# A fused attention, gated convolution and spatial-gating kernel: two token tiles of batch 1 are loaded in long rows and transposed by TensorE, the rest in 32 small loads, under a new order

## The chip, the cores and the metric

One core of a Trainium2 chip. The metric is the device time of one execution in microseconds (us); for the kernel before it is given as the median of three runs. One more execution of it was profiled, and every duration below is from that one.

## The reference

q, k and v are (4, 8, 576, 64) in batch, head, token and head dimension. Three layers follow one another, all in fp32:

```python
scores = scale * np.matmul(q, k.transpose(0, 1, 3, 2))
mask = (rel >= 0) & (rel < 64)          # rel = query position - key position
attn = softmax(np.where(mask, scores, -1000000000.0))
x = np.matmul(attn, v)                  # heads joined: (4, 576, 512)

h = np.maximum(x @ w_in, 0.0)           # 512 -> 1024
conv_out = 3-tap convolution of h along the tokens
x = (h * sigmoid(conv_out)) @ w_out     # 1024 -> 512

h = np.maximum(x @ w2_in, 0.0)          # 512 -> 1024, split into u and v
v_s = np.einsum('ts,bsd->btd', w_spatial, layernorm(v)) + b_spatial[None, :, None]
out = (u * v_s) @ w2_out                # 512 -> 512
```

## The kernel before

Products are done in three matmuls each, of high and low parts of the two factors. The work comes in this order of stages, which overlap:

- Attention runs in 18 rounds (`rec_round`), each of two blocks of 64 queries; batch 0 has blocks 0 to 8, so round 4 holds the last block of batch 0 and the first of batch 1. A round is: scores `s` (L625; in the first six rounds the mask is added by two matmuls of L620), row maxima on DVE, exponentials on ACT (L654), normalisation, transposes `pt` (L684) and their copies `pts`, and `pv` (L717), whose result is split into the high and low parts `xc`.
- The 2304 tokens of x form six chunks of 384. Chunk c needs rounds up to 3c + 2. For each there are eight groups `h` (L810 to L812, 12 matmuls of 386 or 388 columns each) and eight groups `y` (L882 to L884). w_in and w_out come in blocks through two `raw` buffers and are converted on DVE and ACT.
- The second layer follows in the last part, batch by batch; there `gr` is multiplied (L1186 on DVE, L1189 on POOL).

q and k must lie with the head dimension on partitions. Batch 0 gets there by `rec_load_first` and `rec_qk_first`: a tile of 128 tokens is loaded in rows of 256 B into a stage buffer `qk` (five of them; four issues of 128 KB for q and k), and TensorE transposes it (four matmuls `tr` of L556 for q and four for k), with a copy out of PSUM for each. Batches 1 to 3 use `rec_load_qk` (L533): eight loads of 288 KB, in pieces of 128 B, followed by 32x32 transposes on DVE (`rec_qk`, L570), two for each pair of blocks. v comes in windows of 128 tokens (`rec_load_v`, L544), into three buffers `vw`.

Nothing is written in program order. Each `op` has a rank, a cost for each engine that may do it, and at times an earliest time `at`; the class `Plan` runs a list schedule over these numbers and emits the instructions in the order that comes out, which is then fixed for each engine's queue. DMAs are all issued by SP, in that order too, and an issue whose buffer is not free holds up those behind it. The ranks come from the table `PLAN`. The earliest time is the last argument here:

```python
op(rank + 0.1 * g, {"D": 2.5}, ld, w=[(nm, b, "ld", g)], b=[dst[b]], at=rank)
```

`bias(k, t)` weighs the engines against each other by two times, TE1 and TE2, of the schedule.

Of the kernel before, what the change touches and what calls it, by code (L numbers as in the profile page):

```python
# [20 lines left out]
PLAN = {  # L21
    "BP": 0.532,
    "BP1": 0.052,
    "BP2": 2.886,
    "BV": 1.453,
    "BV1": 2.001,
    "BV2": 2.211,
    "CS": 1.104,
    "CW": -3.463,
    "CWL": 0.128,  # L30
    "DC": 1.72,
    "G2S": -0.157,
    "G2": 5.836,
    "LAT": 0.209,
    "LD0": 3.993,
    "LD": 1.243,
    "LEAD": 1.994,
    "PORT": 0.05,
    "QK": -1.46,
    "QL": 0.083,  # L40
    "QL1": -7.091,
    "QV": 1.784,
# [22 lines left out]
    "wo0": 7.827,
    "wo1": -9.101,
    "wo2": -13.346,
    "wo3": 15.676,
    "wo4": -39.117,
    "wo5": -20.38,  # L70
    "wo6": 10.642,
    "wo7": 8.186,
    "r0": -5.237,
    "r1": 29.482,
    "r2": -6.678,
    "r3": -1.91,
    "r4": -2.742,
    "r5": -40.242,
    "r6": 7.708,
    "r7": 7.596,  # L80
    "r8": -0.104,
    "r9": -4.244,
    "r10": -0.595,
    "r11": -29.119,
    "r12": -9.391,
    "r13": -0.755,
    "r14": -10.067,
    "r15": -19.207,
    "r16": -13.345,
    "r17": -2.471,  # L90
# [161 lines left out]
def tile_attention_convglu_spatial(  # L252
# [261 lines left out]
    def rec_load_first(t, rank):  # L514
# [33 lines left out]
    def rec_qk_first(t, rank):  # L548
        n = min(P, S - t * P)
        for j, (nm, dst) in enumerate((("q", qT[0]), ("k", kT[0]))):  # L550
            a = stage[t]
# [5 lines left out]
            key = (nm, "tr", t)  # L557
            op(rank, {"T": 0.46}, tr, r=[("qk0", t, j), "ident"], w=[key], b=[a, pt_])
# [3 lines left out]
                r=[key], w=[(nm, 0, 2 * t + i) for i in range(n // W)], b=[pt_, dst],  # L562
            )

    def rec_qk(b, i, n, rank):

        for nm, dst in (("q", qT[b]), ("k", kT[b])):
            def tr(e, dst=dst):
                d = dst()[:, :, i * W:(i + n) * W]
                nc.vector.transpose(out=d, in_=d.rearrange("p h (u c) -> p h u c", c=32))  # L570
            op(
                rank, {"V": c_tt(n * W * HP)}, tr,
                r=[(nm, b, "ld", g) for g in range(4)], w=[(nm, b, i + j) for j in range(n)], b=[dst],
            )
# [29 lines left out]
    def rec_round(p, rank):  # L604
# [134 lines left out]
    def rec_conv(rank, load, n, issues=1, lead=PLAN["LD"], ring=None):  # L739

        raw = ring or mk(p2, [P, n, 2], I, "raw", "raw", 2)
# [5 lines left out]
        op(rank - lead, {"D": PLAN["DC"]}, lambda e: load(raw()), w=[(key, "raw")], b=[raw], issues=issues)  # L747
# [24 lines left out]
    def rec_w_in(f, rank):  # L772
# [6 lines left out]
        get, own, key, _ = rec_conv(rank, ld, KD * P, issues=2, lead=PLAN["LD0"] if f < 2 else PLAN["LD"])  # L779
# [150 lines left out]
    for t in range(NT):  # L930
        rec_load_first(t, t_block(0, 2 * t) - (PLAN["QL1"] if t else 12.0))
# [6 lines left out]
    for t in range(NT):  # L938
        rec_qk_first(t, t_block(0, 2 * t) - PLAN["QK"])
# [378 lines left out]
```

## Time and profile before

| | |
|---|---|
| median of 3 runs | 532.07 us (531.66 to 533.03) |
| profiled execution | 535.2 us, of which 533.4 us are the span of its instructions |
| mean granted clock of TensorE | 0.955 |
| busy: PE, DVE, ACT, POOL | 507.0, 348.4, 292.8, 36.6 us (95%, 65%, 55%, 7%) |
| moved by DMA | 67.99 MB, 127 GB/s on average |

PE is TensorE's matmuls, DVE is VectorE, ACT is ScalarE, POOL is GpSimd, and SP is the engine that issues the DMAs; "SPq" in a row is an issue. A busy share is an average over the span. L12 is line 12 of the kernel. The granted clock is a share of TensorE's full 2.4 GHz, so 0.50 is its lower level.

### The profile page before, as it was taken

Reading aid. Unit: us, or ns where it says so; the run is one execution under the profiler, and the core shown is the slowest. Engines: PE = TensorE matmul, PEld = TensorE weight load, DVE = VectorE, ACT = ScalarE, POOL = GpSimd, SP = SyncE. Lnnn points to the kernel's source line nnn. Section 1 sums busy time; section 2 is a strip of 40 time slices with the busy share of each in tenths; the row PEclk is TensorE's granted clock in tenths of the full one; section 3 lists DMA queues with packets and bytes.
Section 4 is the critical chain, followed back from the end, with each engine's and each line's share of the span. In section 5 each row is a group of like instructions: output and inputs, shape, how many; then the busy total and the mean of one; then the engine's idle time right before and its main releaser. Section 6 shows DMA issues by size and latency. Waiting matters only on the chain.

```text
span 533.4 us, 10143 instructions
## 1 busy us (share of the span) xinstructions
PE 507.0 (95%) x3826; PEld 466.5 (87%) x3826; DVE 348.4 (65%) x925; ACT 292.8 (55%) x783; POOL 36.6 (7%) x74
## 2 busy tenths in 40 slices
PE   5774799999999999999999999999999999999997
PEld 4543699999999999999999998998899889988996
DVE  3477899999889888975765428987207820771170
ACT  4576799899878977885544225724220432042111
POOL 3000000000000000000000000051004000400130
PEclk9565699999999999999999999999999999999999
DMA  9999859944997856232346752550222021402003
GB/s 184 168 162 196 202 167 144 205 120 126 156 210 201 247 172 194 60 96 80 80 139 209 254 189 64 178 179 2 79 73 107 0 80 35 163 2 79 1 1 98
DMA packets 133077, 67.99 MB, mean 127 GB/s; under 512 B 106828, under 2 KB 119396, under 8 KB 133028
## 3 DMA queue, kind: packets, MB, share of 16 engines
q1 hardware_dynamic: 133028, 67.35, 52.5%
q8 instruction: 30, 0.49, 0.4%
q14 instruction: 19, 0.16, 0.1%
HBM read 48.98 MB, written 18.35 MB: 126 GB/s over the span
## 4 chain that ended last, share of the span: by engine, by line
PE 89%; SPq 3%; DMA 3%; ACT 3%; DVE 2%; issue 1%; ACTq 0%
PE y L882 7%; PE h L810 7%; PE h L811 6%; PE y L883 6%; PE h L812 6%; PE y L884 6%; PE s L625 4%; PE pv L717 3%; PE sps L1173 3%; PE sps L1172 3%; PE sps L1174 3%; PE ops L1227 3%; PE ops L1225 3%; PE ops L1226 3%; PE vps L1049 3%; PE vps L1051 3%
## 5 line engine op out<-in xcount | busy, mean ns | idle before, releaser
L810 PE MATMUL h<-xc,wi 128*128 128x388 f32 (+1 forms) x192 | 67.5, 351 | 0.0
L882 PE MATMUL y<-g,wo 128*128 128x386 f32 (+1 forms) x192 | 67.3, 350 | 0.0
L842 DVE SCALAR_TENSOR_TENSOR cv<-hs,cw,cv 128x386 f32<-128x386 f32 (+1 forms) x96 | 57.7, 612 | 14.1 <-ACT cv L837 13.7
L811 PE MATMUL h<-xc,wi 128*128 128x388 f32 (+1 forms) x192 | 65.3, 340 | 0.0
L883 PE MATMUL y<-g,wo 128*128 128x386 f32 (+1 forms) x192 | 65.2, 340 | 0.0
L812 PE MATMUL h<-xc,wi 128*128 128x388 f32 (+1 forms) x192 | 65.0, 339 | 0.0
L884 PE MATMUL y<-g,wo 128*128 128x386 f32 (+1 forms) x192 | 64.9, 338 | 0.0
L1186 DVE TENSOR_TENSOR gr<-sps,bb 128x288 f32<-128x288 f32 x32 | 14.6, 457 | 68.7 <-PE sps L1178 67.3
L1110 PE MATMUL ups<-yt,w2i 128*128 128x288 f32 x128 | 38.0, 297 | 0.2 <-DVE ut L358 0.2
L1111 PE MATMUL ups<-yt,w2i 128*128 128x288 f32 x128 | 37.8, 295 | 0.0
L654 ACT ACTIVATE sm<-sm,st 128x128 f32<-128x128 f32 x96 | 37.1, 392 | 1.1 <-DVE st L644 1.1
L882 PEld LDWEIGHTS y<-g,wo 128*128 128x128 f32 x192 | 36.1, 188 | 1.8 <-issue 1.2
L1112 PE MATMUL ups<-yt,w2i 128*128 128x288 f32 x128 | 37.7, 294 | 0.0
L810 PEld LDWEIGHTS h<-xc,wi 128*128 128x128 f32 x192 | 36.2, 188 | 1.0 <-issue 0.5
L884 PEld LDWEIGHTS y<-g,wo 128*128 128x128 f32 x192 | 36.4, 190 | 0.0
L1189 POOL TENSOR_TENSOR gr<-gr,ut 128x288 f32<-128x288 f32 x31 | 26.6, 858 | 141.0 <-DVE gr L1186 140.4
L883 PEld LDWEIGHTS y<-g,wo 128*128 128x128 f32 x192 | 36.2, 189 | 0.0
L811 PEld LDWEIGHTS h<-xc,wi 128*128 128x128 f32 x192 | 36.2, 189 | 0.0
L812 PEld LDWEIGHTS h<-xc,wi 128*128 128x128 f32 x192 | 36.2, 188 | 0.0
L356 ACT ACTIVATE hs<-h 128x388 f32<-128x388 f32 (+1 forms) x45 | 21.7, 490 | 25.7 <-PE h L812 24.9
L684 PE MATMUL pt<-ident,sm 128*128 128x128 f32 x144 | 24.9, 300 | 9.6 <-DVE sm L674 5.0
L684 PEld LDWEIGHTS pt<-ident,sm 128*128 128x128 f32 x144 | 18.9, 153 | 13.0 <-ACT sm L654 5.1
(164 smaller groups left out, 1285.4 us busy)
## 6 DMA issues: line engine op xcount, KB each, us to landing
yt<-yd SPq DMA_DIRECT2D x32, 288.0 KB, 5.2
vw<-in_v_dram SPq DMA_DIRECT2D x32, 256.0 KB, 4.0
raw<-in_moe_w_out_dram SPq DMA_DIRECT2D x12, 512.0 KB, 4.5
raw<-in_moe_w_in_dram SPq DMA_DIRECT2D x16, 256.0 KB, 4.9
raw<-in_moe_w_in_dram SPq DMA_DIRECT2D x8, 512.0 KB, 4.9
w2i<-w2d SPq DMA_DIRECT2D x8, 512.0 KB, 7.1
out_dram<-osb SPq DMA_DIRECT2D x15, 256.0 KB, 2.0
qT<-in_q_dram SPq DMA_DIRECT2D x12, 288.0 KB, 7.0
```

The source lines that it names most:

```text
L654: nc.scalar.activation(out=sm[h]()[:, hp, :], in_=src()[:, hp, :], func=ACTF.Exp, scale=scale if early else -1.0, bias=st()[:, 0, h, hp:hp ...
L684: nc.tensor.transpose(psp[h]()[:, hp, :], sm[h]()[:, hp, :], ident)
L810: mm(hps(), wh, xh, start=(kk == 0), stop=False)
L811: mm(hps(), wh, xl, start=False, stop=False)
L812: mm(hps(), wl, xh, start=False, stop=(kk == KD - 1))
L842: return lambda e: nc.vector.scalar_tensor_tensor(out=cv(), in0=h()[:, j:j + n], scalar=cw[:, j, f:f + 1], in1=cv(), op0=ALU.mult, op1=ALU.add
L882: mm(yps(), wt[:, 0], gt[:, 0, :], start=(kk == 0), stop=False)
L883: mm(yps(), wt[:, 0], gt[:, 1, :], start=False, stop=False)
L884: mm(yps(), wt[:, 1], gt[:, 0, :], start=False, stop=(kk == KF - 1))
L1110: mm(ups(), wt[:, 0], yt[b][0]()[:, kk, o], start=(kk == 0), stop=False)
L1111: mm(ups(), wt[:, 0], yt[b][1]()[:, kk, o], start=False, stop=False)
L1112: mm(ups(), wt[:, 1], yt[b][0]()[:, kk, o], start=False, stop=(kk == KD - 1))
```

## The change

The first two tiles of 128 tokens of batch 1 go the way of batch 0 (`FIRST1 = 2`). The other 320 tokens of batch 1 are loaded head by head, in 32 loads of 40 KB, at the earliest at the rank plus `Q1`; two of the five pairs of DVE transposes of batch 1 fall away. Costs that the schedule counts with are changed (a load of a q and k tile or a v window 1.2 to 1.35, of a batch 2.5 to 2.8, of a w_in block 1.72 to 2.1, the maxima of a late round 1.46 to 0.85). All other numbers of `PLAN` are replaced as well, so that the order changes everywhere; with TE2 at 2057 the bias `BIAS2` holds in the whole schedule, and 31 multiplications of `gr` and three subtractions of w2_out leave POOL. W2 at 181.8 puts the conversions of w2_in at a late rank. The lines of before are found 3 to 17 further down in the code after (L533 as L543 and L548, L556 as L573, L570 as L587, L625 as L642, L684 as L701, L717 as L734, L810 as L827).

```diff
     "DC": 1.72,
...
-    "LD": 1.243,
-    "QK": -1.46,
-    "TE2": 333.331,
-    "W2": 5.115,
...
+    "LD": 7.632,
+    "QK": -0.385,
+    "QL2": 3.737,
+    "QK2": 1.454,
+    "Q1": -0.389,
+    "TE2": 2057.37,
+    "W2": 181.82,
...
+    FIRST1 = 2
+
+    def rec_load_first(b, t, rank):
...
-                        out=a()[:n, j, :, h], in_=src[0, h * HP:(h + 1) * HP, t * P:t * P + n, :].rearrange("h p d -> p h d")
+                        out=a()[:n, j, :, h], in_=src[b, h * HP:(h + 1) * HP, t * P:t * P + n, :].rearrange("h p d -> p h d")
...
-            op(rank + 0.01 * j, {"D": 1.2 * n / P}, ld, w=[("qk0", t, j)], b=[a], issues=2)
+            op(rank + 0.01 * j, {"D": 1.35 * n / P}, ld, w=[("qk0", b, t, j)], b=[a], issues=2)
...
+        t0 = FIRST1 * P if b == 1 else 0
         for nm, src, dst in (("q", q, qT), ("k", k, kT)):
             for g in range(4):
...
+                for hp in range(HP if t0 else 1):
+                    def ld(e, src=src, dst=dst, g=g, hp=hp):
+                        part = src[b, 4 * (g // 2):4 * (g // 2) + 4, :, 32 * (g % 2):32 * (g % 2) + 32]
+                        d = dst[b]()[32 * g:32 * g + 32]
+                        if t0:
+                            nc.sync.dma_start(
+                                out=d[:, hp, t0:].rearrange("p (u c) -> p u c", c=32),
+                                in_=part[hp, t0:].rearrange("(u t) c -> t u c", t=32),
+                            )
+                        else:
+                            nc.sync.dma_start(
+                                out=d.rearrange("p h (u c) -> p (h u) c", c=32), in_=part.rearrange("h (u t) c -> t (h u) c", t=32)
+                            )
+                    op(
+                        rank + 0.1 * g, {"D": 0.45 if t0 else 2.8}, ld, w=[(nm, b, "ld", g, hp)], b=[dst[b]],
+                        at=rank + (PLAN["Q1"] if t0 else 0.0),
                     )
-                op(rank + 0.1 * g, {"D": 2.5}, ld, w=[(nm, b, "ld", g)], b=[dst[b]], at=rank)
...
-            rank, {"D": 1.2},
+            rank, {"D": 1.35},
...
-                rank + 1 * rs + 0.1 * h, {"V": 0.85 if early else 1.46}, mx(h),
+                rank + 1 * rs + 0.1 * h, {"V": 0.85}, mx(h),
...
-        get, own, key, _ = rec_conv(rank, ld, KD * P, issues=2, lead=PLAN["LD0"] if f < 2 else PLAN["LD"])
+        get, own, key, _ = rec_conv(rank, ld, KD * P, issues=2, lead=PLAN["LD0"] if f < 2 else PLAN["LD"], dc=2.1)
...
+    for t in range(FIRST1):
+        rec_load_first(1, t, t_block(1, 2 * t) - PLAN["QL2"])
...
+    for t in range(FIRST1):
+        rec_qk_first(1, t, t_block(1, 2 * t) - PLAN["QK2"])
...
-            if b and i % 2 == 0:
+            if b and i % 2 == 0 and (b > 1 or i >= 2 * FIRST1):
                 rec_qk(b, i, min(2, NB - i), t_round[p] - PLAN["QV"] + 0.1 * i)
```

How the rows of the engines stand now: first PE around rounds 4 and 5, up to the first h of chunk 0. `s` with a mask are scores, `qk_266` and `qk_438` are the two stage buffers of batch 1, and `qk_387` is batch 0's last tile. Before, the rows there are these:

```order
L684 MATMUL pt<-ident,sm 128x128 x4
L620 MATMUL s<-mask_84,ident_r 128x512 x2
L625 MATMUL s<-kT,qT 64x128 x16
L717 MATMUL pv<-pts,vw 64x64 x16
L684 MATMUL pt<-ident,sm 128x128 x8
L717 MATMUL pv<-pts,vw 64x64 x16
L620 MATMUL s<-mask_82,ident_r 128x512 x2
L625 MATMUL s<-kT,qT 64x128 x16
L684 MATMUL pt<-ident,sm 128x128 x4
L810 MATMUL h<-xc,wi_313 128x386
```

and of the change:

```order
L701 MATMUL pt<-ident,sm 128x128 x4
L573 MATMUL tr<-ident,qk_266 128x128 x4
L573 MATMUL tr<-ident,qk_387 128x64 x4
L573 MATMUL tr<-ident,qk_438 128x128 x4
L573 MATMUL tr<-ident,qk_266 128x128 x4
L573 MATMUL tr<-ident,qk_438 128x128 x4
L637 MATMUL s<-mask_84,ident_r 128x512 x2
L642 MATMUL s<-kT,qT 64x128 x16
L734 MATMUL pv<-pts,vw 64x64 x16
L701 MATMUL pt<-ident,sm 128x128 x8
L637 MATMUL s<-mask_82,ident_r 128x512 x2
L642 MATMUL s<-kT,qT 64x128 x16
```

Four groups of batch 1's transposes have come in ahead of round 4's scores. Between the scores of rounds 4 and 5 there stood two pv, of rounds 1 and 2; now there is one, of round 2, since that of round 1 has moved further ahead. The row behind those of the change is the first `h`; the pt that stood ahead of it now stands among chunk 0's h.

Second, PE where chunk 0's h end and chunk 1's begin (386 columns are chunk 0's, 388 chunk 1's). Before:

```order
L810 MATMUL h<-xc,wi_595 128x386
L811 MATMUL h<-xc,wi_595 128x386
L812 MATMUL h<-xc,wi_595 128x386
L810 MATMUL h<-xc,wi_313 128x388
L811 MATMUL h<-xc,wi_313 128x388
L812 MATMUL h<-xc,wi_313 128x388
```

and of the change:

```order
L829 MATMUL h<-xc,wi_746 128x386
L701 MATMUL pt<-ident,sm 128x128 x4
L642 MATMUL s<-kT,qT 64x128 x16
L734 MATMUL pv<-pts,vw 64x64 x16
L701 MATMUL pt<-ident,sm 128x128 x4
L734 MATMUL pv<-pts,vw 64x64 x16
L701 MATMUL pt<-ident,sm 128x128 x4
L642 MATMUL s<-kT,qT 64x128 x16
L701 MATMUL pt<-ident,sm 128x128 x4
L827 MATMUL h<-xc,wi_341 128x388
```

The scores of rounds 6 and 7 (without a mask matmul) and pv of rounds 4 and 5 have moved between the two chunks; before, pv of rounds 4 and 5 stood among chunk 0's h, and the scores of round 6 behind two groups of chunk 1.

Third, SP, the queue of DMA issues, around the last of batch 1's loads. Before:

```order
L533 DMA kT<-in_k_dram 32x72x32
L533 DMA qT<-in_q_dram 32x72x32
L775 DMA raw<-in_moe_w_in_dram 64x4x256 x2
L533 DMA kT<-in_k_dram 32x72x32
L775 DMA raw<-in_moe_w_in_dram 64x4x256 x2
L544 DMA vw<-in_v_dram 128x8x64 x3
L775 DMA raw<-in_moe_w_in_dram 64x4x256 x4
L544 DMA vw<-in_v_dram 128x8x64 x2
L737 DMA raw<-in_moe_w_out_dram 128x1024 x2
```

and of the change, from the v windows that follow pv of round 2 on:

```order
L561 DMA vw<-in_v_dram 128x8x64 x2
L792 DMA raw<-in_moe_w_in_dram 64x4x256 x4
L543 DMA qT<-in_q_dram 32x10x32 x4
L543 DMA kT<-in_k_dram 32x10x32 x4
...
L754 DMA raw<-in_moe_w_out_dram 128x1024 x2
L561 DMA vw<-in_v_dram 128x8x64 x3
```

The eight large loads of batch 1, which began ahead of most of w_in, have become 32 small ones (four times the pair of rows shown) behind all of w_in and behind the v windows that wait for pv of round 2; the window that pv of round 4 reads is the first of the last row.

## Rows read from the trace of the kernel before

**Rows 1.** Busy tenths, clock and DMA in 40 slices of 13.3 us
```profile
PE   5774799999999999999999999999999999999997
...
PEclk9565699999999999999999999999999999999999
...
DMA  9999859944997856232346752550222021402003
```

**Rows 2.** Windows; PEclk is the granted clock, then DMA share and GB/s
```profile
8.00:16.00 8.00, 1.81 (x25) 1.09 (x17) 4.92 (x17) 5.68 (x23) 0.00 (x0) 0.72 1.31 212
...
33.45:40.68 7.23, 5.66 (x44) 3.60 (x43) 5.53 (x16) 5.70 (x27) 0.00 (x0) 0.50 1.41 146
...
60.00:66.00 6.00, 5.91 (x70) 4.59 (x70) 4.83 (x13) 5.78 (x18) 0.00 (x0) 0.50 0.83 242
...
66.00:120.00 54.00, 54.00 (x488) 51.40 (x488) 51.28 (x124) 50.16 (x130) 0.32 (x2) 1.00 0.87 159
...
490.00:533.40 43.40, 40.31 (x271) 37.95 (x269) 11.02 (x28) 7.48 (x18) 6.76 (x8) 1.00 0.11 37
```

**Rows 3.** PE's timeline: start and length in us, line, count, wait before
```profile
14.20 1.09 PE L684 MATMUL pt<-ident,sm 128*128 128x128 f32 x4 [5.01 <-DVE sm L674]
...
19.83 1.11 PE L556 MATMUL tr<-ident,qk 128*128 128x128 f32 x4
...
25.41 1.99 PE L625 MATMUL s<-kT,qT 64*64 64x128 f32 x32
...
33.45 1.99 PE L625 MATMUL s<-kT,qT 64*64 64x128 f32 x32
...
40.68 1.99 PE L625 MATMUL s<-kT,qT 64*64 64x128 f32 x32
...
52.66 2.15 PE L625 MATMUL s<-kT,qT 64*64 64x128 f32 x30 [4.61 <-DVE kT L570]
...
66.52 0.42 PE L810 MATMUL h<-xc,wi 128*128 128x386 f32 x1
...
89.16 0.34 PE L810 MATMUL h<-xc,wi 128*128 128x388 f32 x1
```

**Rows 4.** SP's timeline of DMA issues: start and length in us
```profile
4.33 0.61 SPq L461 DMA_DIRECT2D cwr<-in_moe_conv_w_dram  x1
...
18.25 0.50 SPq L533 DMA_DIRECT2D qT<-in_q_dram  x1
...
56.29 1.00 SPq L544 DMA_DIRECT2D vw<-in_v_dram  x2
...
175.64 0.33 SPq L995 DMA_DIRECT2D w2d<-raw  x1
```

**Rows 5.** Groups on ACT by form, 0 to 200 us
```profile
L340 ACT ACTIVATE pts<-pt 128x512 f32<-128x512 f32 x25 | 14.9, 597 | 4.0 <-PE pt L684 3.8
...
L340 ACT ACTIVATE g<-cv 128x768 fp32r<-128x768 f32 x6 | 4.9, 838 | 0.1
```

**Rows 6.** Groups on DVE by form, 0 to 200 us
```profile
L570 DVE STREAM_TRANSPOSE qT<-qT 128x512 f32<-128x512 f32 x12 | 8.2, 693 | 0.0
```

**Rows 7.** DMA issues from 0 to 30 us: size, median us to landing
```profile
qk<-in_q_dram SPq DMA_DIRECT2D x8, 128.0 KB, 3.5
...
qk<-in_q_dram SPq DMA_DIRECT2D x2, 64.0 KB, 3.9
```

**Rows 8.** Chain that ended last, in order of time: start, us, what
```profile
37.11 2.80 ACT sm L654 x16
...
66.76 0.18 PE h L810
...
68.88 1.08 PE pv L717 x32
...
72.29 0.44 PE pt L684 x4
```

**Rows 9.** Costliest groups, from the page
```profile
L1189 POOL TENSOR_TENSOR gr<-gr,ut 128x288 f32<-128x288 f32 x31 | 26.6, 858 | 141.0 <-DVE gr L1186 140.4
```

More of the change, by code (lines that the diff above doesn't have):

```diff
@@ L21 @@
 PLAN = {
[L22 to L30, printed above, removed]
+    "BP": 2.193,
+    "BP1": 0.136,
+    "BP2": 6.659,
+    "BV": 6.821,
+    "BV1": 2.092,
+    "BV2": 2.577,
+    "CS": 0.05,
+    "CW": 0.773,
+    "CWL": -0.949,
     "DC": 1.72,
-    "G2S": -0.157,
-    "G2": 5.836,
+    "G2S": 2.346,
+    "G2": 0.114,
     "LAT": 0.209,
-    "LD0": 3.993,
-    "LD": 1.243,
-    "LEAD": 1.994,
@@ L65 @@
[L65 to L90, printed above, removed]
+    "LD0": 1.137,
@@ new lines @@
+    "LD": 7.632,
+    "LEAD": 1.661,
+    "PORT": 9.641,
+    "QK": -0.385,
+    "QL2": 3.737,
+    "QK2": 1.454,
+    "Q1": -0.389,
+    "QL": -3.131,
+    "QL1": -4.129,
+    "QV": 2.046,
+    "RD": 2.215,
+    "RS": 0.282,
+    "SW": 0.683,
+    "TA": -1.01,
+    "TE1": -2.386,
+    "TE2": 2057.37,
+    "TL": 1.458,
+    "TR": 11.837,
+    "VL": -17.199,
+    "W2": 181.82,
+    "WI": -1.539,
+    "WIS": -11.479,
+    "WO": 1.811,
+    "WOS": -0.777,
+    "wi0": -20.317,
+    "wi1": 8.242,
+    "wi2": 25.498,
@@ new lines @@
+    "wi3": 1.985,
+    "wi4": 9.571,
+    "wi5": -4.58,
+    "wi6": -22.33,
+    "wi7": -26.966,
+    "wo0": 8.495,
+    "wo1": 12.269,
+    "wo2": 11.028,
+    "wo3": 8.527,
+    "wo4": -13.159,
+    "wo5": -16.166,
+    "wo6": 0.498,
+    "wo7": 15.742,
+    "r0": -7.992,
+    "r1": -1.549,
+    "r2": -8.829,
+    "r3": 6.779,
+    "r4": 0.271,
+    "r5": 19.857,
+    "r6": 7.176,
+    "r7": 0.17,
+    "r8": -6.257,
+    "r9": -2.701,
+    "r10": -10.53,
+    "r11": -11.632,
+    "r12": 20.106,
@@ L91 @@
+    "r13": -4.502,
+    "r14": -12.785,
+    "r15": -5.409,
+    "r16": 6.72,
+    "r17": 0.443,
 }
@@ L512, in tile_attention_convglu_spatial @@
     stage, vw = {}, {}
-    def rec_load_first(t, rank):
+    FIRST1 = 2
+    def rec_load_first(b, t, rank):
         n = min(P, S - t * P)
@@ L546, in rec_load_v, with rec_qk_first @@
         )
-    def rec_qk_first(t, rank):
+    def rec_qk_first(b, t, rank):
         n = min(P, S - t * P)
-        for j, (nm, dst) in enumerate((("q", qT[0]), ("k", kT[0]))):
-            a = stage[t]
+        for j, (nm, dst) in enumerate((("q", qT[b]), ("k", kT[b]))):
+            a = stage[b, t]
             pt_ = ps("y", [P, HP, P], "tr")
@@ L556, in tr @@
                     nc.tensor.transpose(pt_()[:, hp, :n], a()[:n, j, hp].rearrange("p h d -> p (h d)"), ident[:n, :n])
-            key = (nm, "tr", t)
-            op(rank, {"T": 0.46}, tr, r=[("qk0", t, j), "ident"], w=[key], b=[a, pt_])
+            key = (nm, b, "tr", t)
+            op(rank, {"T": 0.46}, tr, r=[("qk0", b, t, j), "ident"], w=[key], b=[a, pt_])
             op(
@@ L561, in rec_qk_first @@
                 lambda e, pt_=pt_, dst=dst: copy_to(e, dst()[:, :, t * P:t * P + n], pt_()[:, :, :n]),
-                r=[key], w=[(nm, 0, 2 * t + i) for i in range(n // W)], b=[pt_, dst],
+                r=[key], w=[(nm, b, 2 * t + i) for i in range(n // W)], b=[pt_, dst],
             )
@@ L572, in rec_qk @@
                 rank, {"V": c_tt(n * W * HP)}, tr,
-                r=[(nm, b, "ld", g) for g in range(4)], w=[(nm, b, i + j) for j in range(n)], b=[dst],
+                r=[(nm, b, "ld", g, hp) for g in range(4) for hp in range(HP if b == 1 else 1)], w=[(nm, b, i + j) for j in range(n)], b=[dst],
             )
@@ L737, in plain, with rec_conv @@
         return lambda raw: nc.sync.dma_start(out=raw.rearrange("p c w -> p (c w)"), in_=src)
-    def rec_conv(rank, load, n, issues=1, lead=PLAN["LD"], ring=None):
-        raw = ring or mk(p2, [P, n, 2], I, "raw", "raw", 2)
+    def rec_conv(rank, load, n, issues=1, lead=PLAN["LD"], dc=PLAN["DC"]):
+        raw = mk(p2, [P, n, 2], I, "raw", "raw", 2)
         u = mk(p2, [P, n], I, "wu", "wu", 1)
@@ L746, in rec_conv @@
         key = ("w", len(plan.ops))
-        op(rank - lead, {"D": PLAN["DC"]}, lambda e: load(raw()), w=[(key, "raw")], b=[raw], issues=issues)
+        op(rank - lead, {"D": dc}, lambda e: load(raw()), w=[(key, "raw")], b=[raw], issues=issues)
         op(
```

35 lines of the change are left out of this document (3 added, 32 removed).

## Prediction

> **What bounds the kernel now.** I read the page's second part first, because it shows where TensorE is not busy. PE stands at 9 tenths in every slice but the first five and the last, its clock row is at 5 or 6 tenths in just those early slices, and the DMA row is at 8 or 9 until the sixth slice [rows 1]. So everything that can be won or lost lies before about 66 us, or in new holes made after it. The windows put numbers on it: from 66 to 120 us PE is busy 54.00 of 54.00 us at clock 1.00, and DVE (51.28) and ACT (50.16) are nearly full too, at 95% and 93%; at 60 to 66 PE is busy 5.91 of 6 us but at clock 0.50 [rows 2]. Then the timeline of PE, for what it does before 66 us: the scores of the rounds start at 25.41, 33.45 and 40.68, 7 to 8 us apart; those of round 4, the first that touches batch 1, run at 52.66 after a wait of 4.61 us for the 32x32 transposes of batch 1's k; the first h (L810) is at 66.52, and the first h of chunk 1 at 89.16, directly behind chunk 0's [rows 3]. From 66.5 us on the time is TensorE's work, so the change is worth the amount by which that work ends its start-up earlier, less what new holes cost.
>
> **The change part by part.**
>
> *Loads ahead of round 4.* Removed: eight loads of batch 1's q and k, 288 KB each (2.36 MB), which before begin at 18.25 [rows 4]. In their place come 8 issues of 128 KB (1.05 MB) early, and 32 of 40 KB (1.31 MB) late. At the 212 GB/s of 8 to 16 us [rows 2] the early ones are 4.9 us of transfer, and 8 issues of 0.5 to 0.61 [rows 4] are 4.4 us of SP. So round 4 waits for 1.05 MB and not for 2.36 MB, and the wait of 4.61 us should go. What is late next there is the round itself.
>
> *Transposes.* 16 more on PE, four groups of four at 1.11 each at half clock [rows 3] = 4.4 us, say 4.2 as some run faster; four PSUM copies at 0.60 on ACT [rows 5] or as long on DVE, against four stream transposes of 0.69 fewer on DVE [rows 6]: nothing there.
>
> *First h of chunk 0.* PE's order up to it has the same rounds as before. In after the transposes of the second token tile stand ahead of round 0's pt, and no w_in scaling stands ahead of round 0's exponentials on ACT; the first pt was at 14.20 before [rows 3] and I put it at 13.3, so round 1's scores start at 14.8 after 1.1 of pt and the masks. Four rounds up to round 5's scores at 7.6 each (the mean of the two intervals above, 8.0 and 7.2) are 30.4; the transposes 4.2; the scores themselves 2.0: 51.4. All of that is at the half clock of 33 to 41 us [rows 2]; with PE less idle some of it will be faster, and I take **50** instead of 66.5. Bounds: a round is at least ACT's 5.70 busy us between 33.45 and 40.68 [rows 2], which with transposes at full clock gives 14.8 + 22.8 + 2.1 + 1 = 41, and I use 45 as the low end since the rounds never yet ran at ACT's bound; 8.0 per round and a landing of 4 us [rows 7] that is waited for once give 56.
>
> *Chunk 1's first h.* This is the place that decides. In after it no longer follows chunk 0's directly: a pt, the scores of round 6, pv of round 4, pt, pv of round 5, pt, the scores of round 7 and a pt stand between. Round 6 needs the late pieces of batch 1; pv of round 4 needs a v window whose load stands on SP behind all 32 pieces. Step by step:
> - pv of round 2 ends about 5 us ahead of the first h (between them the scores 2.0, masks and two pt of 1.1), at 45. SP's next v loads wait for it, as there are 3 such buffers. They (two, 0.5 each [rows 4]) and two w_in blocks (four issues of 0.6 and an estimated 1.3 of waiting for a raw buffer) take SP to 50.
> - 32 pieces: the trace has no 40 KB piece. The nearest row is the 0.50 of a single issue of the same load; bounds are 0.33 (a single w2d issue) and 0.61 (the 24 KB conv weights) [rows 4]. 16 us (10.6 to 19.5): SP is free at 66, the last piece landed at about 68.5.
> - Two w_out blocks and the v window, 1.31 MB at 212 GB/s = 6.2 us, and 2.3 of latency: the window is there at 75.
> - PE meanwhile: eight h of 12 matmuls at 0.175 = 2.1 each, 16.8; one pv 1.08; three pt of 0.44 [rows 8]: from 50 free at 69.2. On DVE the two stream transposes (0.69 each [rows 6]) stand with a g and three steps of the convolution around them, some 2.6 us after the last landing: scores of round 6 at 71 to 72, then pv of round 4 at 75 to 76.1.
> - Behind it on ACT: xc 0.6, four exponentials 1.4 (16 instructions of eight took 2.80 [rows 8]), pts 0.6, g 0.84 [rows 5], exponentials 1.4: 80.9. On DVE the reciprocals and, an estimate from the count of instructions at 0.69, 3.7 of transposes and w_out work stand up to the subtraction that finishes round 5's xc. **Chunk 1's first h at 85.**
>
> *The lead.* The same PE work in before: 66.5 plus eight h 16.8, three pv 3.24, six pt 2.64 and two scores 2.07 = 91.3. So after is 6.3 ahead there. But between 69 and 85 PE has only some 5 us of work. The row of 60 to 66 shows PE all but full at 0.50 after a stretch of waits, and the next row 1.00 [rows 2]; a second start of that kind costs 6 us at half clock, 3 us (bounds 0 and 3: the granted clock may also stay at 1.00). Lead 3.3.
>
> *After 85 us.* DVE's 95% leaves little to catch up: one stall of 1 us (0 to 4, the holes a full DVE could leave over two chunks). Lead 2.3. POOL's 31 multiplications of the last stages (0.858 each, 26.6 us [rows 9]) and three subtractions of w2_out go to DVE and ACT. Between 490 and 533, where the last of them stand, DVE is busy 11.02 of 43.40 us [rows 2]; even all 26.6 would fit into what is free, so they hide. Without that cover, the last one alone would cost its 0.86 at the end. The conversions of w2_in, now at the lowest rank, lie under stages in which PE is full [rows 1]: 0.
>
> Sum: 66.5 - 50 = 16.5 won at the first h, 10.2 lost again up to chunk 1, 3 by the clock, 1 by stalls: **-2.3**. The profiled execution took 535.2 (533.4 of span and 1.8 around it), 3.1 above the median; the difference is applied to the median, 532.07 - 2.3 = **529.8**.
>
> **The rivals.**
> A. The forecast, own range 526 to 533 from the bounds of the clock and stalls: 0.38.
> B. The lead stays. Pieces issue at 0.33 and first h is at 45: pv of round 2 at 40, SP through the pieces at 55.6, v window at 64, PE free at 64, chunk 1's first h near 78: lead 13, less 3 and 1: -9 (-6 to -12), 523. For it speaks that idle SP issues at 0.33; against it that the one single issue of a q load in the rows took 0.50. 0.20.
> C. The change does not do what it says: the early rounds are set by ACT and the half clock, not by loads. First h at 53 to 54, pv of round 2 at 48.5, window at 78.5, chunk 1 at 88.5: 2.8 - 3 - 1, so 0 within 1.6. For it speaks that rounds 2 and 3 were 7.2 apart though all of batch 0's loads were issued before 18.25. 0.16.
> D. Slower: round 4's pv waits behind the pieces. At 0.61 each and first h at 56, pv of round 2 ends at 51, SP gets through at 75.5, the window lands at 84.5, chunk 1's first h is at 94.5: 3.2 late, with the clock's 3 some +6 (+2 to +8), 538. It decides once chunk 1's first h is later than 91.3 - 3 = 88.3. For it speaks that SP's own rows reach 0.61 for a small issue and that 16 us of issue stand in front of a load that PE waits for; against it that the pieces could start well before PE is done with chunk 0. 0.26.
> On D the Trainium skill has a rule against this change: "DMA: Bandwidth & Descriptors", section "Rules for kernel authors", says that many small transfers should be joined into a large one, since under 64 KB one pays mostly overhead; a piece here is 40 KB. By that rule the 32 pieces would be nearer to D than to B. The trace leans the same way: a 64 KB load of q landed after 3.9 us, where one of 128 KB took 3.5 [rows 7], so that the smaller gains no time; it shows no piece as small as 40 KB.
>
> **How the numbers follow.** What a measurement of this kernel can tell from no change is about 0.3%, 1.6 us. A gives 0.24 faster, 0.10 same, 0.04 slower; B 0.20 faster; C 0.02 faster, 0.11 same, 0.03 slower; D 0.01 same, 0.25 slower: faster 0.46, same 0.22, slower 0.32. The range reaches from B's better half to D's price, 521.5 to 537.5; outside are the ends of B and D, about 2 in 10.
>
> **What would show it.** Right: no wait of PE for DVE kT in round 4; first h of chunk 0 between 45 and 56; the pieces on SP near 50 to 66 at 0.5; chunk 1's first h near 85, with PE waiting for round 4's v window and then for ACT, and a clock of 0.5 behind it. Wrong: PE full up to chunk 1's first h (then B); a piece above 0.6, or the first h after 56 (then D); new waits of PE between 90 and 200, which would say that my 1 us for a full DVE is too little; or PE waiting on DVE in the last 43 us.

## The result, and the profile after

The changed kernel takes 526.61 us (median of four runs, 525.84 to 527.75) against 532.55 for the kernel before on the same chip (531.66 to 535.13): a ratio of 0.9889, with a 95% interval of 0.9863 to 0.9915. That is 5.9 us less, inside the range of 521.5 to 537.5 and on the side that was forecast, but 3.2 below the 529.8 predicted. The profiled execution took 526.51, of which 524.6 are the span.

The page's second part of the kernel after, in slices of 13.1 us, answers to [rows 1]:

```profile
PE   6877959999999999999999999999999999999997
...
PEclk9798967999999999999999999999999999999999
```

PE is at 6 to 9 tenths in the first five slices, where it was at 4 to 7, but its sixth slice is down to 5: there is a hole that was not there before, and the clock's row has a 6 in the same slice. The windows (length, busy PE, PEld, DVE, ACT, POOL with counts, clock, DMA share, GB/s) place it, as [rows 2] did for before:

```profile
33.00:45.00 12.00, 7.92 (x97) 5.65 (x96) 11.40 (x30) 11.01 (x44) 0.00 (x0) 0.92 1.10 208
60.00:66.00 6.00, 6.00 (x36) 5.96 (x35) 5.83 (x10) 4.41 (x9) 0.00 (x0) 1.00 0.54 90
66.00:75.00 9.00, 4.19 (x69) 3.28 (x67) 8.53 (x22) 7.84 (x20) 0.00 (x0) 0.74 0.70 192
75.00:90.00 15.00, 13.32 (x135) 11.71 (x136) 14.10 (x52) 13.45 (x43) 0.00 (x0) 0.70 0.49 142
90.00:120.00 30.00, 30.00 (x229) 29.38 (x228) 26.57 (x63) 26.09 (x62) 0.51 (x2) 1.00 1.12 196
120.00:200.00 80.00, 80.00 (x743) 75.84 (x742) 71.88 (x214) 59.52 (x182) 0.32 (x2) 1.00 0.68 146
```

Between 60 and 66 us PE is full at full clock already; between 66 and 75 it has 4.19 us of work in 9, while DVE is busy 8.53 of them; between 75 and 90 the clock is at 0.70 on average; and from 90 on PE is full again at 1.00, with no wait in 30 and in 80 us. The timeline of PE (start, length, line, count, and what it waited for) gives the steps, for [rows 3]:

```profile
14.89 1.99 PE L642 MATMUL s<-kT,qT 64*64 64x128 f32 x32
...
37.68 1.10 PE L642 MATMUL s<-kT,qT 64*64 64x128 f32 x32
...
46.75 0.44 PE L827 MATMUL h<-xc,wi 128*128 128x386 f32 x1
...
65.93 0.60 PE L701 MATMUL pt<-ident,sm 128*128 128x128 f32 x4
...
68.33 1.28 PE L642 MATMUL s<-kT,qT 64*64 64x128 f32 x30 [1.45 <-DVE kT L587]
...
70.92 1.76 PE L734 MATMUL pv<-pts,vw 128*64 128x64 f32 x28 [1.04 <-DMA vw<-in_v_dram]
...
75.45 1.11 PE L701 MATMUL pt<-ident,sm 128*128 128x128 f32 x4 [2.77 <-ACT pts L343]
...
78.20 1.97 PE L734 MATMUL pv<-pts,vw 128*64 128x64 f32 x30 [1.23 <-ACT pts L343]
...
83.83 0.53 PE L827 MATMUL h<-xc,wi 128*128 128x388 f32 x1
```

Round 1's scores are at 14.89 (25.41 before), those of round 4 at 37.68 and without a wait for DVE's 32x32 transposes (52.66 before), chunk 0's first h is at 46.75 (66.52). Then comes the hole, from the end of chunk 0's h at 65.9: four waits of 1.45, 1.04, 2.77 and 1.23 us, the last instructions at 2 us where full clock takes 1.1, and chunk 1's first h at 83.83 (89.16). SP's timeline shows where the small loads stand, for [rows 4]:

```profile
46.13 2.11 SPq L543 DMA_DIRECT2D qT<-in_q_dram  x4
...
58.00 1.97 SPq L543 DMA_DIRECT2D kT<-in_k_dram  x4
...
62.02 2.20 SPq L543 DMA_DIRECT2D kT<-in_k_dram  x4
...
65.29 7.59 SPq L561 DMA_DIRECT2D vw<-in_v_dram  x3
```

The 32 small loads begin at 46.13 and end at 64.2, four in 2.11 to 2.93 at first and in 1.97 later, which is 0.50 apiece. The view of DMA issues from 30 to 90 us gives their landing, for [rows 7]:

```profile
qT<-in_q_dram SPq DMA_DIRECT2D x16, 40.0 KB, 2.1
```

The chain that ended last, in order of time, through the hole (start, length, what):

```profile
65.29 5.59 DMA vw<-in_v_dram
...
73.39 1.53 ACT sm L671 x8
...
74.91 0.48 ACT pts L343
...
76.13 1.54 ACT sm L671 x8
```

The window for round 4's pv is the last thing that SP releases in this execution, at 70.9 (in another one of the same kernel pv does not wait for it: see after_again below). From there on the chain is ACT's own order: the copies pts of round 5 stand behind four exponentials of round 6 each time (1.53 and 1.54), then come pv, pt, the scores of round 7 and a pt on PE, at half clock.

**The lead, by equal work.** Up to chunk 1's first h PE has done in after all that it had done in before at 89.16, and two scores (1.03 each) and two pt (0.44) more, besides batch 1's transposes: the same point in before is 92.1. So the lead there is 8.3 us. At the last matmul it is 9.1 (530.3 against 521.2); where the 0.8 between the two comes from is not shown. The pair of executions that was profiled differs by 8.7 and the medians by 5.9: the profiled execution of before ran at 535.2, 2.7 above its median, so some 2.7 of the lead belongs to that execution and not to the change. The executions of before lie between 530.5 and 535.2 in all, those of after between 525.0 and 527.9.

### The profile page after: what moved, and what is told of

It is laid out like the page before. It is cut to its first block, busy times and chain, and to the rows that moved or that the text cites. A ratio compares the mean times of both kernels' runs of the same rounds, so it can differ in the third digit from the quotient of the medians.

```text
span 524.6 us, 10177 instructions
## 1 busy us (share of the span) xinstructions
PE 502.8 (96%) x3842; PEld 465.4 (89%) x3842; DVE 350.4 (67%) x943; ACT 297.3 (57%) x802; POOL 6.1 (1%) x40
## 4 chain that ended last, share of the span: by engine, by line
PE 88%; ACT 5%; SPq 3%; DMA 2%; DVE 1%; issue 1%; POOL 0%; POOLq 0%
PE y L899 7%; PE y L900 6%; PE y L901 6%; PE h L827 6%; PE h L828 5%; PE h L829 5%; PE pv L734 3%; PE ups L1131 3%; PE ups L1132 3%; PE sps L1193 3%; PE sps L1195 3%; PE sps L1194 3%; PE ups L1133 3%; PE ops L1248 3%; PE ops L1247 3%; PE ops L1246 3%
## 5 line engine op out<-in xcount | busy, mean ns | idle before, releaser
L827 PE MATMUL h<-xc,wi 128*128 128x388 f32 (+1 forms) x192 | 66.9, 349 | 0.0
L343 ACT ACTIVATE gd<-gr 128x224 fp32r<-128x224 f32 (+1 forms) x31 | 12.9, 417 | 46.0 <-DVE gr L1210 46.0
L827 PEld LDWEIGHTS h<-xc,wi 128*128 128x128 f32 x192 | 36.3, 189 | 1.2 <-issue 0.7
L701 PE MATMUL pt<-ident,sm 128*128 128x128 f32 x144 | 25.1, 302 | 8.8 <-ACT pts L343 3.5
L359 ACT ACTIVATE ut<-ups 128x288 f32<-128x288 f32 x31 | 12.6, 409 | 29.4 <-PE ups L1133 29.4
```

What stands on the lines that cost most here:

```text
L359: nc.scalar.activation(out=out_, in_=in_, func=ACTF.Relu)
L827: mm(hps(), wh, xh, start=(kk == 0), stop=False)
```

## The experiments

The theory behind the prediction was that the new loads bring round 4 forward (theory L or N below), and that the small loads and the window behind them then set the hole (P). The rivals were that the new order alone brings the gain (O), and that the hole is a matter of ACT and DVE (C, V, A). A letter here is that of the expectation quoted beside it; where one of the prediction's rivals A to D is meant, the text says so. Ratios are to the kernel before on the same chip, the changed kernel's own being 0.9889.

**load_only: the loads without the order.** The numbers and costs of before, with these three added and the code of the change:

```diff
+    "QL2": 8,
+    "QK2": 1.454,
+    "Q1": 12,
```

> The kernel before with its own numbers and costs, and only the new loads: batch 1's first two tiles in long rows and transposed by TensorE, its other 320 tokens in 32 small loads (lead of the tile loads 8, earliest time of the small ones 12 after their rank, so that they stand behind the tiles). Theory L (the gain is that round 4 waits for 1.05 MB of batch 1 and not for 2.36 MB): the 4.6 us wait of round 4's scores is gone, chunk 0's first h comes at 54 to 60 instead of 66.5, and the time is 2 to 7 us below before. Rival O (the gain is in the new order, the loads alone bring nothing): within 1.6 us of before, or slower.

543.29 us, ratio 1.0196 (1.0165 to 1.0227): slower by 11. Its PE timeline:

```profile
30.14 1.44 PE L642 MATMUL s<-kT,qT 64*64 64x128 f32 x32
...
59.64 1.76 PE L734 MATMUL pv<-pts,vw 128*64 128x64 f32 x28 [4.57 <-DMA vw<-in_v_dram]
...
65.09 0.42 PE L827 MATMUL h<-xc,wi 128*128 128x386 f32 x1
```

Round 4's scores no longer wait for DVE, as expected; but round 1's scores stand at 30.14, a v window that stands behind the small loads on SP makes pv wait 4.57, and chunk 0's first h is at 65.09, hardly earlier than before. Further on PE is busy only 7.88 of 10 us from 110 to 120. Theory L falls for the order that these numbers make.

**load_late: the same, the small loads further back.**

```diff
-    "Q1": 12,
+    "Q1": 30,
```

> The kernel before with its own numbers and the new loads once more, now with the 32 small loads behind all w_in blocks on SP (earliest time 30 after their rank), as they stand in the changed kernel; PE keeps the rounds and the h of chunks 0 and 1 in nearly the order of before. In the first trial the small loads held up the v windows and w_in. Theory L2 (the loads help by themselves once the small ones do not stand ahead of what chunk 0 needs): chunk 0's first h at 52 to 58, time 524 to 530. Rival B (loads and order only work together): 533 or more.

545.05 us, ratio 1.0225 (1.0195 to 1.0255). Its PE timeline:

```profile
67.73 1.76 PE L734 MATMUL pv<-pts,vw 128*64 128x64 f32 x28 [3.36 <-DMA vw<-in_v_dram]
```

The wait for a window is still there, as the windows stand behind the small loads whichever place these have, and chunk 0's first h comes at 71.52. Rival B was right: the loads alone bring nothing under the old numbers.

**plan_only: the numbers without the loads.**

```diff
-    FIRST1 = 2
+    FIRST1 = 0
```

> The changed kernel with all its numbers and costs, but batch 1 loaded as before (eight loads of 288 KB, all its transposes on DVE). The order follows from the same numbers, so round 4 now stands behind chunk 0's h. Theory L: without the tile loads round 4 is late again and chunk 1's h has to wait for it; 530 to 540 us. Rival O: the numbers carry the gain, 525 to 529.

544.0 us, ratio 1.0194 (1.015 to 1.0238). Its PE timeline:

```profile
15.29 1.73 PE L642 MATMUL s<-kT,qT 64*64 64x128 f32 x32
...
39.63 0.67 PE L827 MATMUL h<-xc,wi 128*128 128x386 f32 x1
...
74.69 2.15 PE L642 MATMUL s<-kT,qT 64*64 64x128 f32 x30 [10.77 <-DVE kT L587]
...
106.52 0.69 PE L827 MATMUL h<-xc,wi 128*128 128x388 f32 x1
```

Round 1's scores are at 15.29, so that part of the gain is the order's and needs no new load. The first h is even at 39.63, because round 4 has moved behind chunk 0's h; but there it waits 10.77 us for DVE and batch 1, and chunk 1 begins at 106.52. Rival O falls; the loss foreseen by theory L is there and larger than its 530 to 540.

**order_kept: the new order step for step, the old loads.** The three trials above let the schedule form anew. Here every instruction keeps its place, the four pairs of tile loads become the eight loads of 288 KB, the small loads and batch 1's transposes on TensorE are left out, and DVE transposes in place of the copies:

```diff
+                if b == 1:
+                    d_ = (qT, kT)[j][b]()
+                    for g in (2 * t, 2 * t + 1):
+                        part = src[b, 4 * (g // 2):4 * (g // 2) + 4, :, 32 * (g % 2):32 * (g % 2) + 32]
+                        nc.sync.dma_start(
+                            out=d_[32 * g:32 * g + 32].rearrange("p h (u c) -> p (h u) c", c=32),
+                            in_=part.rearrange("h (u t) c -> t (h u) c", t=32),
+                        )
+                    return
...
```

> The changed kernel in its own order, with batch 1 loaded as before the change: the eight loads of 288 KB stand on SP where the four pairs of tile loads stood, the 32 small loads are left out, the 16 transposes on TensorE are left out, and four 32x32 transposes on DVE stand in place of the four copies out of PSUM. So the order is the new one and the loads are the old ones; 2.36 MB instead of 1.05 MB stand ahead of the last part of batch 0 and of the v windows. 1.31 MB more at 212 GB/s are 6.2 us: chunk 0's first h at 51 to 55 instead of 46.8. Theory N (the new loads are needed): round 4 waits for DVE's transposes again, the lead at chunk 0 is not won back, chunk 1's first h at 87 or later, time 529 to 535. Rival E (with 16 us less of small loads on SP the v window and round 6's tokens are there early, and the chain of ACT from pv of round 4 on ends at the same time): chunk 1's first h at 83 to 86, time 525 to 528.

537.92 us, ratio 1.0102 (1.0085 to 1.012), 11.3 above the changed kernel and 5.9 above before. Its PE timeline, and two rows of SP's:

```profile
31.26 1.09 PE L586 MATMUL tr<-ident,qk 128*128 128x128 f32 x4 [5.87 <-DMA qk<-in_q_dram]
...
49.81 2.16 PE L657 MATMUL s<-kT,qT 64*64 64x128 f32 x30 [5.95 <-DVE kT L591]
...
59.48 0.69 PE L842 MATMUL h<-xc,wi 128*128 128x386 f32 x1
...
79.55 0.60 PE L716 MATMUL pt<-ident,sm 128*128 128x128 f32 x4
...
96.33 0.42 PE L842 MATMUL h<-xc,wi 128*128 128x388 f32 x1
```

```profile
14.81 5.33 SPq L530 DMA_DIRECT2D qT<-in_q_dram  x2
20.19 4.11 SPq L530 DMA_DIRECT2D kT<-in_k_dram  x2
```

Four loads of 288 KB hold SP from 14.81 to 24.30; batch 0's third tile stands behind them, and its transposes wait 5.87 us. Then round 4 waits 5.95 for DVE. Chunk 0's first h is at 59.48, 12.7 later and not 6.2 as I had worked out from bytes alone, since two waits follow from one queue. So with this order the new loads are needed: theory N holds, with a larger loss than its 529 to 535. It holds for the eight large loads in this place; another place for them, behind batch 0's tiles, was not tried. The trial shows one thing more. There are no small loads here and no wait for a window, the last of batch 1's loads has landed by 49.03, and no DMA runs from 73 to 79 us. Still round 6's scores wait 1.44 for DVE (1.45 in the changed kernel), and from the pt at 79.55 to chunk 1's h at 96.33 it takes 16.8 us, against 17.9 (65.93 to 83.83) in the changed kernel. The hole is there without the small loads and the window behind them.

**early8: eight small loads ahead of the windows.** Only SP's order is changed:

```diff
+        seq = [o for o in order if o[2] in self.pieces][:8]
+        order = [o for o in order if o not in seq]
+        at7 = [x for x, o in enumerate(order) if o[2] in self.windows][6]
+        order[at7:at7] = seq
...
```

> The changed kernel in its own order on every engine, but the first 8 of the 32 small loads stand on SP ahead of the two v windows that wait for pv of round 2, where SP idles from about 37 to 40 us. The other 24 then end some 4 us earlier. Theory P (the hole of TensorE between 66 and 84 us is set by the small loads and the v window behind them): the waits of round 6's scores for DVE (1.4) and of round 4's pv for its window (1.0) go, and the time is 1.5 to 3 us below the changed kernel. Rival C (the hole is set by the chain of exponentials, copies and DVE work behind): within 0.8 of it.

528.19 us (527.96 to 528.31), ratio 0.9913 (0.9884 to 0.9942): its runs lie above all those of the changed kernel, by 1.6 in the median, but the intervals of the two ratios overlap. Both expectations missed: chunk 1's first h is at 85.79. A row of ACT's timeline looked like the reason:

```profile
51.18 0.68 ACT L348 ACTIVATE wt<-raw 128x512 f32<-128x512 f32 x1 [2.36 <-DMA raw<-in_moe_w_in_dram]
```

A block of w_in landed late, ACT stood 2.36 us in front of it with the relu of an h queued behind, and PE waited 1.87 for that. The wait for the window did go, but the pt behind it waited 4.1 for its copy instead of 2.8. None of this can be put down to the eight loads, though: a second profile of the changed kernel (after_again below), with nothing moved, has the same three, at 2.30, 1.79 and 4.24, and no wait for the window either. What moving eight loads forward costs is not shown.

**keep_clock: TensorE kept busy in the hole.**

```diff
+    def fill(n):
+        t_ = ps2.tile([P, P], F, tag="y", name="fill", bufs=2)
+        for _ in range(n):
+            nc.tensor.transpose(t_, ident, ident)
...
+            if p == 6:
+                fill(8)
...
+                if (p, h) == (5, 1):
+                    fill(14)
...
+            if p in (4, 5):
+                fill(6)
```

> The changed kernel, its order unchanged, with 34 extra transposes of the identity (their result is not used) put on TensorE where it waits in the hole between 66 and 84 us: 8 ahead of round 6's scores, 6 ahead of pv of round 4, 14 ahead of the pt behind it, 6 ahead of pv of round 5. Theory K (the half clock of 70 to 84 us costs time, as the last pv, pt and scores run at 2 us instead of 1.1): the granted clock stays near 1.00, chunk 1's first h comes 1 to 2.5 us earlier, time 524 to 525.5. Rival V (DVE's last subtraction of xc, at 81.95 to 82.64, sets the end of the hole): chunk 1's first h at 83 or later, time within 0.8 of the changed kernel, or above by the extra work.

525.78 us (524.44 to 527.31), ratio 0.9872 (0.984 to 0.9904): not to be told from the changed kernel. Its windows through the hole:

```profile
66.00:75.00 9.00, 7.39 (x101) 6.30 (x100) 9.00 (x22) 8.14 (x21) 0.00 (x0) 1.00 0.74 203
75.00:84.00 9.00, 7.09 (x81) 6.01 (x82) 8.49 (x28) 8.13 (x24) 0.00 (x0) 0.66 0.48 129
```

The clock is at 1.00 up to 75 us, where it had been 0.74 on average, and falls at 77.9; chunk 1's first h is at 84.11. As far as it goes this is rival V: the part of the hole that ran at full clock ended no earlier. But the pieces that theory K names, from pv of round 5 at 78.48 on, still ran at half clock, so the trial does not decide between K and V. The profiled execution is also the slowest of the four.

**pool_g: four subtractions from DVE to POOL.** The low part of chunk 0's g:

```diff
-lambda e: sub_to(e, lo(), src(), hi()),
+lambda e: sub_to("P" if w[:2] == ("g", 0) else e, lo(), src(), hi()),
```

> The changed kernel, its order unchanged, with the four subtractions for the low part of chunk 0's g (0.95 us each on DVE, between 60 and 78 us) on POOL instead. Theory V (DVE, nearly full from 33 to 84 us, sets chunk 1's first h): DVE's last subtraction of xc and with it chunk 1's first h come 1.5 to 3.5 us earlier, time 523 to 525.5. Rival W (the wait goes to the scalar engine and the chain of exponentials, or POOL's own accesses slow DVE down): within 0.8 of the changed kernel.

525.58 us (525.24 to 527.93), ratio 0.9882 (0.9851 to 0.9913). Chunk 1's first h is at 83.14, 0.7 earlier, for 3.7 us taken off DVE. In PE's timeline the wait has gone where rival W put it:

```profile
75.75 1.11 PE L701 MATMUL pt<-ident,sm 128*128 128x128 f32 x4 [3.33 <-ACT pts L343]
```

The pt waits 3.33 for ACT's copy instead of 2.77, and pv of round 5 starts at 78.49, no earlier than in the changed kernel (78.20). The 0.7 comes behind that point: the clock rises again during round 7's scores, which take 1.36 and the pt after them 0.66, where the changed kernel has 1.99 and 1.11. So these four subtractions on DVE, however full it is, do not set the hole.

**first1_5: all of batch 1 by TensorE.** `FIRST1 = 5` and no small loads, under the changed kernel's numbers.

> The changed kernel's code and numbers with all five tiles of batch 1 in long rows and transposed by TensorE: 12 issues more of that kind (10 of 128 KB or 64 KB pairs) and none of the 32 small ones, 24 transposes more on PE in six groups. The order follows anew from the same numbers. Theory P (the 32 small loads, 16 us of SP, are what costs): 522 to 526. Rival N (the numbers fit one set of loads; another set under them makes an order with new waits, as in the two trials above): 530 or more.

536.39 us, ratio 1.0066 (1.0045 to 1.0087). Rival N: the order forms anew, and in it the scores of a round wait for exponentials (ACT sm):

```profile
79.85 0.69 PE L642 MATMUL s<-kT,qT 64*64 64x128 f32 x4 [7.90 <-ACT sm L671]
```

This 7.90 is a new wait in the new order, so the trial says nothing on the price of the small loads.

**pull_r5: round 5 ahead of round 6 on ACT.** Nine steps are moved in an order that is otherwise the same:

```diff
...
+        x5 = ("x", 5, 0)
+        move((("ex", 6, 0),), (("pts", 5, 0),), (("pt", 5, 1),))
+        move((("ex", 6, 1),), (("pts", 5, 1),), (("pv", 5),))
+        move((("rc", 6, 0), ("rc", 6, 1)), ((x5, "h"),), ((x5, "l"),), (("h", 1, 0),), (("h", 1, 1),))
+        move((("pts", 6, 1),), (("hs", 1, 0, 0),))
```

> The changed kernel with nine steps moved in the order and nothing else: on ACT the copies pts of round 5 ahead of the exponentials of round 6 (the first half, and the second half), and round 5's xc ahead of the conversions; its subtraction on DVE ahead of round 6's reciprocals; on PE two h of chunk 1 directly behind pv of round 5, ahead of the pt of round 6 and the scores of round 7. Theory A (the hole of TensorE from 66 to 84 us is set by ACT's order: round 5's copies wait behind round 6's exponentials, 1.5 us each): chunk 1's first h comes 3 to 5 us earlier, at 79 to 81, and the time is 1.5 to 4 us below the changed kernel. Rival V (DVE and ACT are full anyway, what is pulled ahead is paid by what is pushed back): first h earlier, but new waits of PE before 120 us, time within 1 of the changed kernel.

533.17 us (529.11 to 534.57), ratio 1.0011 (0.9978 to 1.0044): 6.7 above the changed kernel beside it (after_again). PE's timeline, a window of the stretch behind, and a row of ACT's timeline:

```profile
78.03 1.97 PE L747 MATMUL pv<-pts,vw 128*64 128x64 f32 x30 [1.84 <-ACT pts L356]
...
80.78 0.66 PE L840 MATMUL h<-xc,wi 128*128 128x388 f32 x1 [0.78 <-ACT xc L356]
...
82.23 0.53 PE L840 MATMUL h<-xc,wi 128*128 128x388 f32 x1
...
93.98 1.88 PE L747 MATMUL pv<-pts,vw 128*64 128x64 f32 x32 [3.50 <-DVE xc L377]
```

```profile
84.00:90.00 6.00, 6.00 (x55) 5.62 (x54) 1.24 (x4) 1.11 (x4) 0.00 (x0) 0.72 0.28 89
```

```profile
88.89 0.60 ACT L356 ACTIVATE pts<-pt 128x512 f32<-128x512 f32 x1 [5.01 <-PE pt L714]
```

Chunk 1's first h is at 80.78, 3.3 earlier than in after_again, but only half of that is theory A's doing. From the pt that opens the hole (67.79) to pv of round 5 (78.03) it takes 10.2 us, where after_again has 11.8: with the copies ahead of the exponentials on ACT that stretch is shorter by the 1.5 us foreseen. The rest comes from the new place of the two h on PE, ahead of round 6's pt and round 7's scores, which is part of the same edit. The gain in time failed by my own placing. The two h ran at half clock (0.53 where full clock takes 0.34) and took 7.5 us and not 4.2; round 6's pt stood behind them, ACT idled 5.01 us in front of the copy of that pt, and from 84 to 90 DVE was busy 1.24 and ACT 1.11 of 6 us. Engines that are full before and after pay such a gap in full: PE then waited 3.50 for xc, and the clock fell again.

**after_again and pool_back.** The changed kernel beside pull_r5, and the changed kernel with the gr multiplications on POOL again (`nc.gpsimd.tensor_tensor` in place of the choice by engine).

> The changed kernel once more, beside the one with the steps moved, for its time on the same chip: 525 to 528, and chunk 1's first h at 83 to 85.

> The changed kernel, its order unchanged, with the multiplications of gr in the second layer on POOL again, as before the change (32 now). The prediction's term was 0, as DVE has room there: within 0.8 of the changed kernel. Rival: DVE's 0.46 each against POOL's 0.86 shortens waits there, so that POOL costs 1 to 3 us.

526.48 us (524.98 to 527.85; ratio 0.9897, 0.9871 to 0.9922), chunk 1's first h at 84.11; and 526.03 us (524.04 to 526.42; ratio 0.9881, 0.985 to 0.9912). For the gr multiplications POOL or DVE makes no difference that can be measured; the term was 0. The three subtractions of w2_out, which the change also moved, were not put back.

The second profile of the changed kernel says more on the hole than its time does. PE's timeline in after_again:

```profile
51.53 0.44 PE L827 MATMUL h<-xc,wi 128*128 128x386 f32 x1 [1.79 <-ACT hs L359]
...
67.95 0.60 PE L701 MATMUL pt<-ident,sm 128*128 128x128 f32 x4
...
71.57 1.15 PE L734 MATMUL pv<-pts,vw 128*64 128x64 f32 x32
...
76.96 1.12 PE L701 MATMUL pt<-ident,sm 128*128 128x128 f32 x4 [4.24 <-ACT pts L343]
...
79.71 1.97 PE L734 MATMUL pv<-pts,vw 128*64 128x64 f32 x30 [1.23 <-ACT pts L343]
...
84.11 0.42 PE L827 MATMUL h<-xc,wi 128*128 128x388 f32 x1
```

The hole has two stretches, from the pt that opens it to pv of round 5, and from there to chunk 1's first h (times in us):

| run | pt | pv of round 5 | first stretch | wait for the window | second stretch |
|---|---|---|---|---|---|
| after | 65.93 | 78.20 | 12.3 | 1.04 | 5.63 |
| after_again | 67.95 | 79.71 | 11.8 | none | 4.40 |
| keep_clock | 66.71 | 78.48 | 11.8 | none | 5.63 |
| order_kept | 79.55 | 91.28 | 11.7 | none | 5.05 |
| pull_r5 | 67.79 | 78.03 | 10.2 | none | its h were moved |

The first stretch takes 11.7 to 11.8 us without a wait for the window, without small loads, or with the clock at 1.00 up to 75 us, and 12.3 with the wait: the window costs some 0.5. Of these runs only the one with another order on ACT is clearly shorter. The second stretch has work of PE in it and no long wait, and it is shorter where the clock is back at 1.00 before round 7's scores are done (after_again, order_kept) and longest where it stays at half up to the h (after, keep_clock).

**before_again: a second profile of before.**

> The kernel before once more, for a second profile: its first one ran at 535.2 us, 3.1 above its median. Theory: the first 66 us vary from execution to execution (clock steps and load times), and everything behind is the same to 0.5 us; then a run near 532 shows chunk 0's first h near 63. Rival: the difference lies behind 66 us, and the first h is at 66 to 67 again.

534.7 us, so again an execution from the upper end. PE's timeline:

```profile
65.37 0.42 PE L810 MATMUL h<-xc,wi 128*128 128x386 f32 x1
...
88.02 0.34 PE L810 MATMUL h<-xc,wi 128*128 128x388 f32 x1
```

Both points are 1.1 us earlier than in [rows 3], and the time is 0.5 less. The trial had wanted a run near 532 and got none, so it does not settle where the 4.7 us between executions of before (530.5 to 535.2) lie.

## Why the prediction was right, step by step

- **Round 4 does not wait.** Right: no wait for DVE's 32x32 transposes in round 4. order_kept shows it by its opposite.
- **First h of chunk 0 at 50.** It came at 46.75, inside the bounds of 45 to 56; 19.8 us were won, not 16.5. The rows split them: round 1's scores came 10.5 earlier (25.41 to 14.89), which is the order's alone (plan_only has 15.29 with the old loads). From round 1 to round 4 it was 22.8 instead of 27.3: about the 4.61 of the wait, though the work in between and the clock differ too. From round 4 to the first h it was 9.1 instead of 13.9, with one pv there and not two. In the sum's own terms, round 1's scores were right (14.8 forecast, 14.89), and the rounds up to round 5's scores with the transposes were mis-sized: 30.4 and 4.2 forecast, 30.1 in all (14.89 to 45.00). The clock was at 1.00 between 19 and 43 us, where I had taken half clock for nearly all of it. The upper bound of 56 adds up to 57 from its terms (14.8, 32, 4.2, 2 and 4), which decides nothing.
- **The small loads.** Taken at 0.5 and 16 us from 50 on; they took 18 from 46.1, at the 0.50 each that was forecast. Their end at 64.2 (66 forecast) was near. 40 KB landed 2.1 us after issue, one load every 0.50 us, so 1.31 MB went at some 80 GB/s, where 33 to 45 us has 208. The Trainium skill says in "DMA: Bandwidth & Descriptors", section "Rules for kernel authors", that under 64 KB one pays mostly overhead; the row agrees. Rival D, which the prediction put beside that rule, did not come about: D wanted chunk 1's first h later than 88.3.
- **Chunk 1's first h at 85.** It came at 83.83, and that it came so near is in part luck, for one step on the way was wrong: I let the window's landing at 75 set it (its terms give 74.5), with ACT's chain behind. The window came at 70.9 and cost some 0.5 us, and order_kept has nearly the same hole with neither small loads nor a late window. What the runs show in its place: up to pv of round 5 the order of exponentials and copies on ACT sets it, of which pull_r5 took 1.5 of some 12 us away; behind pv of round 5 it is PE's own work, longer or shorter by the clock. What holds the other 10 us of the first stretch is read from the profile, where PE's longest wait is for ACT's copies pts (2.77 in after, 4.24 in after_again), and not shown by a trial.
- **The lead of 6.3** was 8.3. I had counted equal work to 91.3 where it is 92.1, and the h came 1.2 earlier than forecast.
- **The clock, 3 us off.** This step failed. I put the half clock behind chunk 1's first h. In after the clock is back at 1.00 from 84.1 on, just as that h begins, and the half clock lay in the hole, under waits and six short pieces of work. Some of its price is inside the 83.83 and so inside the lead: from pv of round 5 to chunk 1's first h after takes 5.63 us, and after_again, where the clock rises on the way, 4.40. pull_r5 shows the price when long work comes first: its two h paid 3.3 us.
- **Later stalls, 1 us off.** None: PE is full from 90 to 120 and from 120 to 200. DVE was busy 26.57 of the 30 us from 90 to 120.
- **POOL's work, 0.** Right for the multiplications, by pool_back.

So the direction and the first steps were right, and in the pair of profiled executions the sum was short by 2.0 of lead and by two terms of loss, 3 and 1, that did not come behind chunk 1's first h: 8.3 there and not 2.3. The medians differ by 5.9, so 2.7 of the pair's difference of 8.7 is the slow profiled execution of before, from whose rows the sum was worked out; which term carries it is not shown. The time lies in the forecast's own range of 526 to 533. Of the prediction's rival B ("the lead stays", 6 to 12 us faster) only the size came near: the small loads issued at 0.5, not 0.33, and PE was not full up to chunk 1's first h. Its rivals C and D did not happen.

What stays open: what sets the rest of the hole's first stretch, how much full clock would take off the second, and why the executions of before are spread over 4.7 us. A fourth v buffer, which would take SP's wait for pv of round 2 away, was not tried.

## What to carry to other kernels

A change of loads and the order that was made for it are one change: here either half alone, with the schedule formed anew, costs 11 to 12 us, the new order kept step for step with the old loads costs 5.9, and both together win 6, so a half that loses in a trial says little about the whole. What a load costs is often paid by the load behind it on the same queue: a v window behind the small loads made pv wait 4.57 in load_only, and a tile behind the large ones made transposes wait 5.87 in order_kept. When a load seems to set a hole, take the load away in an order that is otherwise the same, and look whether the hole stays. And profile the same kernel twice before you explain a wait: here the second profile lost the wait for the window and had the one that early8 seemed to have caused.

## What the runs showed of the hardware

- Four loads of 288 KB in 128 B pieces kept SP issuing from 14.81 to 24.30 in order_kept, where two issues of 128 KB in rows of 256 B take 1.0 to 1.3 us on SP early in the same run. From 14.81 to 24.30 the DMA moved 161 GB/s at a share of 1.14, against 216 at 1.23 from 8 to 16 us. No trial changes the length of the pieces alone.
- Loads of 40 KB went one per 0.50 us and landed after 2.1, at a DMA share of 0.54 from 60 to 66 us of after; SP issued them back to back, so that the issue set their pace and not the transfer.
- The granted clock fell from 1.00 to 0.50 in the hole of after at 70.4 us and came back at 84.1, when the h began; with added transposes (keep_clock) it fell later, at 77.9, and came back at 84.7.
